# The loop order of a two-layer feed-forward stage behind attention and a Fourier mix

## The chip, the cores and the metric

One core of one Trainium2 chip. The metric is the device time in microseconds (us) of one execution. The engines are named as in the profile: PE (TensorE, with PEld for its weight loads), DVE (VectorE), ACT (ScalarE), POOL (GpSimd) and SP (SyncE, which here only issues DMAs). Each engine runs its own instructions in order and waits on semaphores for the others.

## The reference

```python
# q, k, v: (8, 12, 448, 64); w_pre, w_post: (12, 12); w_ch1: (768, 3072); w_ch2: (3072, 768)
scores = (q @ k^T) / 8                                   # per batch and head, 448 x 448
scores = einsum('bhij,hg->bgij', scores, w_pre)          # heads mixed before the softmax
attn = softmax(scores)
attn = einsum('bhij,hg->bgij', attn, w_post)             # and after it
x = (attn @ v) as (8, 448, 768)
u = x + real(fft(fft(x, axis=1), axis=2))
un = (u - mean(u)) / sqrt(var(u) + 1e-6)                 # per row
out = u + relu(un @ w_ch1) @ w_ch2
```

The two weights arrive as 64-bit floats. [...]

## The kernel before, in words

The program has two stages, one after the other.

**The mix** (`mix_phase`) makes u and writes it to DRAM (`u_scr`). Its loop runs over 192 steps, 24 for each batch, and its order on PE and DVE is written out by hand (`tc.manual_schedule`). A step has the premix matmuls (L307, PSUM tile `mx`, one buffer), the row maximum on DVE (L314), the exponential on ACT (L323), a scaling on POOL (L331, L336), the postmix matmuls (L346), a transposing copy on DVE (L357), and in some steps attention times values (L374), the transposes that turn x round (L416), a fold of two row groups on POOL (L431 to L438), and the matmuls of the Fourier transforms (L448, L462), whose results DVE adds onto `X` (L473, L475). Since `mx` has one buffer, the chain premix, maximum, exponential, next premix goes once round in each step. `convert` puts up to four DVE instructions of the weight conversion into each step: a piece is 128 x 384 weights, takes seven instructions (L512 to L523) and is stored to DRAM as `w1f` or `w2f`. There are 96 pieces. `_Evac` deals copies out of PSUM (L128 on ACT, L130 on DVE) to the engine with the smaller sum of estimated work, and each converted piece is charged to DVE there.

**The feed-forward stage** (`ffn_phase`) takes the 3584 rows in seven blocks of 512. Both products use Strassen's scheme: a product of 2 x 2 sub-blocks takes seven products of sums of sub-blocks (the list `ORDER`, with PSUM tiles `psP`, `psQ`, `psR`), so each weight also has sums of its quarters (in the first block made on DVE at L711 and L723 and stored to `w1s` and `w2s`). For each block, `first` runs through the 12 slices of a half of the hidden dimension, two at a time, and loads all of w_ch1 anew; `second` then multiplies the whole hidden activation `h` by all of w_ch2, loaded anew, and adds each finished product onto u (L838). `norm` normalises the next block's u (L746 to L753), transposes it on PE (L759), and POOL makes its sums (L766). A scheduler sets the order in this stage; before its first matmul come the load of u (L693) and `norm` of the first block.

Of the kernel before, what the change touches and what calls it, by code (L numbers as in the profile page):

```python
# [57 lines left out]

WC = 384

TB = 512
NTB = B * S // TB


def _consts():
# [23 lines left out]
    p = np.arange(GR)[:, None, None]  # L89
    at = S * np.arange(B)[:, None] + S - GR * np.arange(2) - p  # L90
    at[0, :, 0] = B * S + np.arange(B)
    return {"at": at.reshape(GR, 2 * B).astype(np.uint32), "ts": ts.astype(np.float32),
# [51 lines left out]

@with_exitstack
def mix_phase(ctx, tc, ident, q, k, v, w_pre, w_post, u_scr, weights):
# [21 lines left out]
    pcv = pool("pcv", 2)  # L168
# [36 lines left out]
    rows = cst.tile([GR, 2 * B], U32, name="rows")  # L205
# [249 lines left out]
    def emit_s2(b, pair, par):  # L455
# [10 lines left out]
        def done():  # L466
# [13 lines left out]
            for back in range(2):  # L480
                X = groups[b * NG + 2 * pair + back].pop("X")
                if back:
                    nc.gpsimd.indirect_dma_start(
                        out=u_scr[:, :],
                        out_offset=bass.IndirectOffsetOnAxis(
                            ap=rows[:GR, 2 * b + pair:2 * b + pair + 1], axis=0),
                        in_=X[:GR, :], in_offset=None)
                    continue
                u0 = b * S + i0
                nc.sync.dma_start(out=u_scr[u0:u0 + GR, :], in_=X[:GR, :])  # L490
                if n > GR:
                    nc.sync.dma_start(out=u_scr[u0 + GR:u0 + n, :], in_=X[GR:n, :])
        return [done]


    def emit_convert(src, r0, c0, dst, split):
        raw = pcv.tile([P, WC, 2], U32, name="raw64", tag="raw64")
        nc.gpsimd.dma_start(
            out=raw.rearrange("p n w -> p (n w)"),
            in_=src[r0:r0 + P, c0:c0 + WC].bitcast(U32))  # L500
        lo, hi = raw[:, :, 0], raw[:, :, 1]
        top = pcv.tile([P, WC], F32, name="top", tag="top")
        tmp = pcv.tile([P, WC], F32, name="tmp", tag="tmp")
        topb, tmpb = top[:, :].bitcast(U32), tmp[:, :].bitcast(U32)

        vec = nc.vector  # L510
        ops = [
            lambda: vec.tensor_scalar(tmpb, hi, 0x7fffffff, None, op0=ALU.bitwise_and),  # L512
            lambda: vec.tensor_scalar(tmp[:, :], tmp[:, :], _f32(0x38000000),
                                      _f32(0x47efffff), op0=ALU.max, op1=ALU.min),
            lambda: vec.tensor_scalar(topb, tmpb, 0x07ffffff, 3, op0=ALU.bitwise_and,
                                      op1=ALU.logical_shift_left),
            lambda: vec.scalar_tensor_tensor(topb, hi, 0xc0000000, topb,
                                             op0=ALU.bitwise_and, op1=ALU.bitwise_or),
            lambda: vec.tensor_scalar(tmpb, topb, 0xff800000, None,
                                      op0=ALU.bitwise_and),  # L520
            lambda: vec.scalar_tensor_tensor(tmp[:, :], lo, 2.0 ** -52, tmp[:, :],
                                             op0=ALU.mult, op1=ALU.mult),
            lambda: vec.tensor_tensor(top[:, :], top[:, :], tmp[:, :], op=ALU.add),  # L523
        ]

        def store():
            ev.d += 7 * 440.0
            nc.sync.dma_start(
                out=dst, in_=top.rearrange("p (m f) -> p m f", m=split))
        return ops, store  # L530

    cuts, conv = list(weights), []

    def convert(n):

        for _ in range(n):
            if not conv and cuts:
# [125 lines left out]
def ffn_phase(ctx, tc, ident, u_scr, w1f, w2f, w1s, w2s, out):  # L663
# [190 lines left out]
    for x in range(NT2):  # L854
        norm(0, x)
# [66 lines left out]
```

## Time and profile before

| | |
|---|---|
| median of 3 runs | 2749.06 us (2737.71 to 2753.45) |
| the profiled execution, its own time | 2746.39 us |
| its span, first to last instruction | 2744.6 us |
| mean granted TensorE clock | 0.967 |
| PE busy | 2476.4 us, 90% of the span |
| DVE busy | 1262.2 us, 46% |
| ACT busy, POOL busy | 724.0 us, 732.0 us |
| moved by DMA | 462.60 MB |

The span has a first part, the mix, in which PE and DVE are both busy over 80% of the time; a short valley between 1065 and 1158 us; and the feed-forward stage, in which PE is busy 98% of the time and DVE about a quarter. A busy share over the whole span says little: each stage has to be read by itself.

### The profile page before, as it was taken

How to read it: one execution, taken by the hardware profiler on the slowest of the kernel's cores; microseconds unless marked ns; L12 is line 12 of the kernel's file. 1: busy time of each engine (PE TensorE's matmuls, PEld its weight loads, DVE VectorE, ACT ScalarE, POOL GpSimd, SP SyncE). 2: the span in 40 equal slices, each digit the busy share in tenths (PEclk: the TensorE clock that was granted, in tenths of full speed). 3: DMA queues.
4: the chain of work that ended last, by engine and by line, in shares of the span. 5: the costliest groups of instructions: out<-in, count | busy, mean ns of one | idle time of the engine just before them, and what ended most of it. 6: DMA issues, size and time to landing. Idle time of an engine off the chain costs nothing.

```text
span 2744.6 us, 46540 instructions
## 1 busy us (share of the span) xinstructions
PE 2476.4 (90%) x18544; PEld 1587.2 (58%) x18544; DVE 1262.2 (46%) x2238; ACT 724.0 (26%) x2135; POOL 732.0 (27%) x1117
## 2 busy tenths in 40 slices
PE   4778888888888886499999999999999999999998
PEld 2334344444444443387577678668658767866865
DVE  3887888888887876543032122213203212221220
ACT  2555555555555552110011001001001100100100
POOL 5465767666665544200100010010010000001000
PEclk7999999999999998799999999999999999999999
DMA  6665657575656457744444444444445444444432
GB/s 168 181 183 173 189 168 202 164 202 164 193 175 186 152 157 252 280 161 175 141 172 165 155 155 161 161 166 161 150 155 171 157 150 167 149 163 160 144 109 107
DMA packets 184471, 462.60 MB, mean 169 GB/s; under 512 B 23111, under 2 KB 129095, under 8 KB 171712
## 3 DMA queue, kind: packets, MB, share of 16 engines
q1 hardware_dynamic: 159968, 361.30, 38.7%
q0 software_dynamic: 24288, 98.33, 13.0%
q8 instruction: 148, 2.42, 0.4%
q14 instruction: 67, 0.55, 0.1%
HBM read 317.17 MB, written 59.79 MB: 137 GB/s over the span
## 4 chain that ended last, share of the span: by engine, by line
PE 41%; issue 9%; DMA 7%; DVE 1%; POOL 0%; SPq 0%; POOLq 0%; ACT 0%
PE psP L829 12%; PE psP L789 10%; PE psR L829 7%; PE psR L789 6%; PE psQ L829 3%; DMA w1t<-w1f 3%; PE psQ L789 2%; DMA u<-u_scr 2%; DMA out_dram<-u 2%; DMA w1t<-w1s 1%; PE psQ L759 1%; DVE st L746 0%; POOL ub L766 0%; DVE u L838 0%; SPq L703 0%
## 5 line engine op out<-in xcount | busy, mean ns | idle before, releaser
L789 PE MATMUL psP<-ub,w1t 128*128 128x256 f32 x2016 | 469.3, 386 | 26.6 <-DVE mv L748 16.9
L789 PEld LDWEIGHTS psP<-ub,w1t 128*128 128x128 f32 x2016 | 385.9, 193 | 94.7 <-DMA w1t<-w1f 22.1
L829 PE MATMUL psP<-w2t,h 128*128 128x384 f32 x1344 | 436.9, 486 | 0.0
L829 PEld LDWEIGHTS psP<-w2t,h 128*128 128x128 f32 x1344 | 254.4, 190 | 173.4
L323 ACT ACTIVATE PP<-mx,nmx 128x448 f32<-128x448 f32 x384 | 239.9, 629 | 376.2 <-DVE nmx L314 372.2
L766 POOL TENSOR_TENSOR ub<-ub 128x768 f32<-128x768 f32 x28 | 50.0, 1806 | 1036.2 <-ACT ub L761 1035.6
L336 POOL TENSOR_SCALAR PP<-PP,rcp 128x448 f32<-128x448 f32 x384 | 259.6, 686 | 154.0 <-DVE rcp L333 109.4
L307 PE MATMUL mx<-Kr,kw 60*64 60x448 f32 x1536 | 204.0, 589 | 97.0 <-ACT PP L323 88.2
L357 DVE STREAM_TRANSPOSE Pv<-po 128x896 f32<-128x896 f32 x192 | 212.9, 1109 | 101.4 <-PE po L346 101.2
L789 PE MATMUL psR<-ub,w1t 128*128 128x256 f32 x1008 | 232.1, 379 | 0.5 <-DMA w1t<-w1s 0.5
L314 DVE TENSOR_REDUCE nmx<-mx 128x2 f32<-128x896 f32 x192 | 206.2, 1074 | 34.9 <-PE mx L307 23.9
L829 PE MATMUL psR<-w2t,h 128*128 128x384 f32 x672 | 220.0, 486 | 0.0
L281 PE MATMUL ms<-kT,qT 64*64 64x448 f32 (+1 forms) x1536 | 205.3, 568 | 7.0 <-DVE X L475 6.3
L374 PEld LDWEIGHTS ms<-Pv,vv 64*64 64x64 f32 x5376 | 169.4, 142 | 67.2 <-issue 38.7
L128 ACT COPY Sb<-ms 124x448 f32<-124x448 f32 x379 | 186.5, 538 | 81.1 <-PE ms L281 66.1
L789 PEld LDWEIGHTS psR<-ub,w1t 128*128 128x128 f32 x1008 | 191.2, 190 | 27.8 <-DMA w1t<-w1s 1.9
L346 PE MATMUL po<-PP,kw 60*32 60x448 f32 x3072 | 194.1, 562 | 9.1 <-DVE rcp L333 7.7
L374 PE MATMUL ms<-Pv,vv 64*64 64x120 f32 x5376 | 181.0, 278 | 16.9 <-ACT Sb L128 15.4
L838 DVE TENSOR_TENSOR u<-u,psP 128x384 f32<-128x384 f32 x56 | 31.0, 554 | 341.6 <-PE psP L829 341.6
L829 PEld LDWEIGHTS psR<-w2t,h 128*128 128x128 f32 x672 | 126.3, 190 | 84.3
L307 PEld LDWEIGHTS mx<-Kr,kw 60*64 60x64 f32 x1536 | 42.2, 135 | 207.1 <-ACT PP L323 153.9
L761 ACT COPY ub<-psQ 128x384 f32<-128x384 f32 x56 | 25.0, 481 | 508.3 <-PE psQ L759 508.3
(92 smaller groups left out, 2604.4 us busy)
## 6 DMA issues: line engine op xcount, KB each, us to landing
Kr<-Sb SPq DMA_DIRECT2D x768, 105.0 KB
w2t<-w2s SPq DMA_DIRECT2D x56, 1152.0 KB
w2t<-w2f SPq DMA_DIRECT2D x42, 1152.0 KB
w1t<-w1s SPq DMA_DIRECT2D x72, 576.0 KB
raw<-in_moe_w_ch_dram POOLq DMA_DIRECT2D x96, 384.0 KB, 4.4
w1t<-w1f SPq DMA_DIRECT2D x84, 384.0 KB
w1t<-w1f SPq DMA_DIRECT2D x96, 192.0 KB
w1t<-w1s SPq DMA_DIRECT2D x72, 192.0 KB
```

Source lines behind the costliest of these rows:

```text
L128: self.nc.scalar.copy(out=out, in_=in_)
L281: nc.tensor.matmul(pss[x][64 * y:64 * y + r0 + 64 - lo, :S], st["qT", xx][64 * x:64 * x + 64, y, lo:r0 + 64], st["kT", xx][64 * x:64 * x + ...
L307: nc.tensor.matmul(mx[64 * z:64 * z + 64, x, :S], kw1[64 * x:64 * x + KR, :], Kr[64 * x:64 * x + KR, z, :], start=True, stop=True)
L314: nc.vector.tensor_reduce(nmx[:, :], steps[T]["mx"][:, :, :S], axis=AX.X, op=ALU.max, negate=True)
L323: nc.scalar.activation(PP[:, x, :], steps[T]["mx"][:, x, :S], ACTF.Exp, bias=steps[T]["nmx"][:, x:x + 1], accum_out=den[:, x:x + 1])
L336: nc.gpsimd.tensor_scalar(PP[:, x, :], PP[:, x, :], rcp[:, x:x + 1], 1.0, op0=ALU.mult, op1=ALU.mult)
L346: nc.tensor.matmul(po[o:o + 32, z, :S], kw2[64 * z:64 * z + KR, y, :], PP[64 * z:64 * z + KR, :, c * HS:(c + 1) * HS], start=True, stop=True)
L357: nc.vector.transpose(g["Pv"][:, T % GT, :].rearrange("p (z s) -> p z s", z=2), steps[T]["po"][:, :, :S])
L374: nc.tensor.matmul(pss[y][64 * x:64 * x + 64, :nu * R], st["v"][64 * y:64 * y + 64, i, jb * D:(jb + 1) * D], _ap(Pv, 64 * y * rp + 32 * jb ...
L766: nc.gpsimd.tensor_tensor(ub[:, o], ub[:, a], ub[:, b], op=ALU.subtract)
L789: nc.tensor.matmul(p, w[m][:, i, kc, :], ub[:, i, kc, :], start=opens and kc == 0, stop=kc == NK - 1, skip_group_check=True)
L829: nc.tensor.matmul(p, lhs[i][:, half * NQ + kf, x * P:(x + 1) * P], w[:, kf, :], start=opens and half == 0 and kf == 0, stop=half == 1 and ...
```

## The change

The feed-forward loop is turned inside out. The hidden dimension is cut into six chunks; the outer loop runs over chunks, the inner one over the seven row blocks, 42 iterations in all. The seven forms of a chunk's weights (three quarters and four sums) lie in SBUF while all seven blocks pass. All of u (seven tiles) stays in SBUF, and each chunk adds its share onto it. The normalised and transposed blocks with their Strassen sums are made during chunk 0, stored to DRAM (`ub_scr`) and loaded again for every later chunk. In the last chunk each finished piece of the output is stored by itself.

The conversion moves with it. In the mix only chunk 0 is converted, at most one DVE instruction a step; the other five chunks are converted during the feed-forward stage, three DVE instructions after each product (`wts.deal(3)`). A unit is one row slice: four raw pieces of seven instructions, four sums, one store. The feed-forward order on PE and DVE is now written out by hand, u has one DRAM tensor for each batch, and its loads are issued by SP and not by POOL.

```diff
+NC = 6
+NM = DFF // 2 // P        # 12
+FM = NM // NC             # 2
+FC = FM * P               # 256
...
+class _Weights:
+    def open(self, ctx, tc):
...
+        self.praw, self.ptmp, self.pst = pool("wraw", 2), pool("wtmp", 1), pool("wst", 1)
...
+        def load(k):          # one raw piece, 256 or 384 weights wide
...
+                nc.gpsimd.dma_start(
+                    out=raws[k][:, :f, :].rearrange("p f w -> p (f w)"),
+                    in_=src.bitcast(U32))
...
+        def begin(k):
...
+            load(k + 1)
...
+        def store():
+            nc.gpsimd.dma_start(out=dst.rearrange("k p f -> p k f"),
+                                in_=box["st"][:, :, :w])
...
+    def deal(self, n):
+        while self.ops and (n > 0 or not self.ops[0][1]):
+            fn, dve = self.ops.pop(0)
+            fn()
+            n -= dve
...
 # the mix
-            ops = 0 if s < -4 else 1 if s - 1 in sums else 4
             if 0 <= s < TOT:
                 emit_postmix(s)
-                convert(min(ops, 1))
+                if s >= 4 and s % GS not in (13, 19, 0, 1):
+                    wts.deal(1)
+                    ev.d += 400.0
                 emit_turn(s)
-                ops -= 1
-            convert(ops)
...
 # the feed-forward stage
-ORDER = (0, 1, 4, 5, 2, 6, 3)
+ORDER = (0, 4, 5, 1, 6, 2, 3)
...
+    def sums(t):
+        for o, a, b in ((4, 6, 0), (5, 2, 4), (6, 2, 6), (3, 1, 5)):
+            nc.vector.tensor_tensor(ubs[t, o][:, :, :], ubs[t, a][:, :, :],
+                                    ubs[t, b][:, :, :], op=ALU.subtract)
+        for i in ORDER:
+            nc.sync.dma_start(out=ub_scr[t][i], in_=ubs[t, i][:, :, :])
...
+    def first(n):
+        c, t = divmod(n, NTB)
...
+            for m in range(FM):
+                for kc in range(NK):
+                    nc.tensor.matmul(p[:, m, :], w1[i][:, kc, m * P:(m + 1) * P],
+                                     ub[:, kc, :],
...
+            if i != 2:
+                wts.deal(3)
+            if t == NTB - 1 and c + 1 < NC:
+                load_w1(c + 1, i)
+            if NTB <= n + 1 < NC * NTB:
+                new_ub(n + 1, i)
+                nc.sync.dma_start(out=ubs[n + 1, i][:, :, :],
+                                  in_=ub_scr[(n + 1) % NTB][i])
...
+    def second(n, h):
...
+        norms = c == 0 and t + 1 < NTB
+        if norms:
+            un = norm(t + 1, 0)
...
+            if norms and k < NT2:
+                turn(t + 1, k, un)
+                if k + 1 < NT2:
+                    un = norm(t + 1, k + 1)
+                else:
+                    sums(t + 1)
+            wts.deal(3)
...
-    for t in range(NTB):
-        if t + 1 < NTB:
-            load_u(t + 1)
-        second(t, first(t))
+    with tc.manual_schedule(engines={mybir.EngineType.PE, mybir.EngineType.DVE}):
+        for n in range(NC * NTB):
+            c, t = divmod(n, NTB)
+            if c + 1 < NC and t < NK + FM:
+                wts.add(c + 1, t)
+            wts.deal(0)
+            if c == 0 and t + 2 < NTB:
+                load_u(t + 2)
+            second(n, first(n))
+            wts.deal(1000)
```

What this does to the order of instructions is seen at three places. The first is DVE in the middle of the mix. Before (L314 is the row maximum, L357 the transposing copy, L333 the softmax's reciprocal, the rest are the conversion):

```order
L333 RECIPROCAL rcp<-den 128x2
L314 TENSOR_REDUCE nmx<-mx 128x2
L523 TENSOR_TENSOR top<-top,tmp 128x384
L357 STREAM_TRANSPOSE Pv<-po 128x896
L512 TENSOR_SCALAR tmp<-raw_922 128x384
L513 TENSOR_SCALAR tmp<-tmp 128x384
L515 TENSOR_SCALAR top<-tmp 128x384
```

and after (a step like it: L441 is the maximum, L484 the transposing copy, L460 the reciprocal, L133 a copy out of PSUM, L219 and L223 the conversion):

```order
L460 RECIPROCAL rcp<-den 128x2
L441 TENSOR_REDUCE nmx<-mx 128x2
L133 COPY Sb<-ms 124x448
L219 TENSOR_SCALAR tmp<-raw_608 128x256
L484 STREAM_TRANSPOSE Pv<-po 128x896
```

Four conversion instructions between one maximum and the next have become one, narrower, and one copy out of PSUM has come over from ACT in some steps.

The second is DVE during `second`. Before, in the second block (h sums L845, additions onto u L838, the last step of `norm` L753; the statistics of `norm` stand earlier, among the instructions of `first`):

```order
L838 TENSOR_TENSOR u<-u,psQ 128x384
L845 TENSOR_TENSOR h<-h 128x1024
L753 TENSOR_SCALAR un<-u,mv,rstd 128x768
L838 TENSOR_TENSOR u<-u,psR 128x384 x2
L753 TENSOR_SCALAR un<-u,mv,rstd 128x768
L838 TENSOR_TENSOR u<-u,psP 128x384 x2
```

and after, in chunk 0 (additions onto u L873, `norm` L775 to L782, conversion L237 to L245):

```order
L873 TENSOR_TENSOR u_13365<-u_13365,psP 128x384 x2
L775 BN_STATS st<-u_13486 128x6 x2
L777 BN_AGGR mv<-st 128x2
L779 TENSOR_SCALAR rstd<-mv 128x1
L782 TENSOR_SCALAR un<-u_13486,mv,rstd 128x768
L237 TENSOR_SCALAR tmp<-wst 128x256
L241 SCALAR_TENSOR_TENSOR tmp<-raw_13784,tmp 128x256
L245 TENSOR_TENSOR wst<-wst,tmp 128x256
L873 TENSOR_TENSOR u_13365<-u_13365,psR 128x384 x2
```

A whole `norm` and three conversion instructions now stand between the additions of one product and those of the next.

The third is SP's queue between the stages. Before, POOL issued the load of u (L693), and SP held loads of w_ch2's pieces (L719, L733) and stores of its sums (L725) among the last stores of u (L490, L492):

```order
L490 DMA u_scr<-X 112x768
L492 DMA u_scr<-X 1x768
L725 DMA w2s<-w2t 128x2x384 x6
L719 DMA w2t<-w2f 128x4x384
L733 DMA w2t<-w2f 128x2304 x3
```

After, the loads of u stand on SP behind two loads of w_ch2's first chunk (`w_0_86`), whose last unit is stored by POOL when DVE has made its last sums at the very end of the mix:

```order
L616 DMA u_72<-X 112x768 x2
L618 DMA u_72<-X 1x768
L760 DMA w2t<-w_0_86 128x768 x2
L751 DMA u_13359<-u_65 128x768 x3
L751 DMA u_13359<-u_65 64x768
L751 DMA u_13359<-u_66 64x768
```

The load of u for block 0 needs only the first two batches (`u_65`, `u_66`), and stands behind a store that comes last.

More of the change, by code (lines that the diff above doesn't have):

```diff
@@ L167, in mix_phase @@
     pzz = pool("pzz")
-    pcv = pool("pcv", 2)
+    wts.open(ctx, tc)
     cst = pool("cst")
@@ L491, in done @@
                 if n > GR:
-                    nc.sync.dma_start(out=u_scr[u0 + GR:u0 + n, :], in_=X[GR:n, :])
+                    nc.sync.dma_start(out=u_scr[b][i0 + GR:i0 + n, :], in_=X[GR:n, :])
         return [done]
[L496 to L537, printed above, removed]
-                ops, store = emit_convert(*cuts.pop(0))
-                conv.extend(ops)
-                conv.append(store)
-            if conv:
-                conv.pop(0)()
-            if len(conv) == 1:
-                conv.pop(0)()
     fill = {"tile": [], "full": [], "none": []}
@@ L552, in mix_phase @@
     LG, LM = 4, 2
-    sums = set()
+    for n in range(NK + FM):
+        wts.add(0, n)
     for b in range(B):
```

360 lines of the change are left out of this document (185 added, 175 removed).

## The prediction

> **What bounds the kernel now.** I read the busy time by stage first, since the page's shares are means over stages with different limits. A row gives a stretch and its length, the busy time of PE, PEld, DVE, ACT and POOL, the granted clock, the DMA share and GB/s.
>
> ```profile
> 52.60:1064.80 1012.20, 856.96 (x12078) 415.56 (x12080) 823.58 (x1350) 556.33 (x1699) 615.97 (x985) 0.96 0.60 178
> 1064.80:1114.90 50.10, 35.58 (x330) 22.17 (x324) 32.48 (x63) 7.72 (x31) 11.25 (x13) 0.82 0.89 300
> 1114.90:1157.50 42.60, 8.64 (x37) 7.02 (x38) 18.55 (x49) 4.10 (x9) 6.50 (x8) 0.56 0.84 309
> 1157.50:2744.60 1587.10, 1551.43 (x6012) 1131.08 (x6011) 375.60 (x747) 146.80 (x383) 72.30 (x64) 0.99 0.45 154
> ```
>
> The first row runs from the first row maximum to the last, 191 step intervals, so 5.30 us a step; PE is idle for 1012.2 - 857.0 = 155.2 us of it, and DVE is busy 81%. The second is the mix's tail, the third the valley until feed-forward matmuls run steadily, the fourth the feed-forward stage, where PE is 98% busy. The change can win at most some 36 us in the fourth row, so the mix and the valley decide. What DVE does for the conversion there:
>
> ```profile
> L521 DVE SCALAR_TENSOR_TENSOR tmp<-raw,tmp 128x384 f32<-128x384 uint32 x95 | 72.2, 760 | 1.4
> L517 DVE SCALAR_TENSOR_TENSOR top<-raw,top 128x384 uint32<-128x384 uint32 x95 | 67.1, 706 | 1.4
> L523 DVE TENSOR_TENSOR top<-top,tmp 128x384 f32<-128x384 f32 x95 | 66.9, 704 | 1.2
> L513 DVE TENSOR_SCALAR tmp<-tmp 128x384 f32<-128x384 f32 x95 | 49.2, 518 | 1.9
> L519 DVE TENSOR_SCALAR tmp<-top 128x384 uint32<-128x384 uint32 x95 | 46.0, 484 | 2.1
> L515 DVE TENSOR_SCALAR top<-tmp 128x384 uint32<-128x384 uint32 x95 | 45.1, 474 | 11.5 <-DMA w1f<-top 9.6 <-DMA w2f<-top 0.9
> L512 DVE TENSOR_SCALAR tmp<-raw 128x384 uint32<-128x384 uint32 x94 | 42.2, 449 | 2.6 <-DMA raw<-in_moe_w_ch_dram 2.6
> ```
>
> Together 388.7 us in 664 instructions, 585 ns each, nearly half of DVE's 823.6. Then what PE waits for there:
>
> ```profile
> L307 PE MATMUL mx<-Kr,kw 60*64 60x448 f32 x1528 | 198.8, 587 | 88.3 <-ACT PP L323 88.2
> ...
> L258 PE MATMUL ms<-ident,rawk 128*128 128x128 f32 x147 | 24.3, 305 | 28.0 <-ACT Sb L128 25.0 <-DMA rawk<-in_k_dram 3.0
> L258 PE MATMUL ms<-ident,rawq 128*128 128x128 f32 x147 | 21.8, 281 | 8.4 <-ACT Sb L128 8.4
> ```
>
> The largest wait is the premix (L307) for the exponential, the chain that goes once round a step; the exponential in its turn waits for the maximum on DVE, which stands behind the conversion. The timeline shows it by the starts of the premix:
>
> ```profile
> 672.56 0.98 PE L307 MATMUL mx<-Kr,kw 60*64 60x448 f32 x8 [0.48 <-ACT PP L323]
> 677.85 0.98 PE L307 MATMUL mx<-Kr,kw 60*64 60x448 f32 x8 [0.58 <-ACT PP L323]
> 683.36 0.98 PE L307 MATMUL mx<-Kr,kw 60*64 60x448 f32 x8 [1.35 <-ACT PP L323]
> ...
> 1025.45 0.98 PE L307 MATMUL mx<-Kr,kw 60*64 60x448 f32 x8
> 1029.50 0.98 PE L307 MATMUL mx<-Kr,kw 60*64 60x448 f32 x8
> ```
>
> Two steps of premix, qk, attention times values and postmix took 5.29 and 5.51 us beside the conversion; one with the same PE work at the end, where the conversion is nearly over, took 4.05. But not every loss is the conversion's:
>
> ```profile
> 972.35 0.98 PE L307 MATMUL mx<-Kr,kw 60*64 60x448 f32 x8 [0.57 <-ACT PP L323]
> ...
> 976.60 0.98 PE L307 MATMUL mx<-Kr,kw 60*64 60x448 f32 x8 [1.60 <-ACT PP L323]
> ...
> 982.33 0.17 DVE L333 RECIPROCAL rcp<-den 128x2 f32<-128x2 f32 x1 [1.76 <-POOL den L331]
> ...
> 984.97 1.77 PE L307 MATMUL mx<-Kr,kw 60*64 60x448 f32 x8 [2.11 <-ACT PP L323]
> ```
>
> Here POOL works on a fold, its `den` comes late, DVE waits in order, and the step takes 8.37 us after one of 4.25.
>
> **The change, part by part.**
>
> *Conversion out of the mix.* 672 instructions become 160, at most one a step: at 585 ns about 300 us leave DVE, which then has some 2.7 us of work in a step and is no bound. What PE gets of it lies between 0 (all waits have other causes) and 155 us (all idle time). The 16 folds stay: 8.37 - 4.25 = 4.1 us each, 66 us. Of the 36.4 us at the transposes (L258), which wait for copies on ACT, I leave half, 18, since ACT gives some copies away but keeps its exponentials. So 155 - 66 - 18 = 71; I take **-70 us**, 4.9 us a step. It agrees with the pairs above: 1.2 to 1.5 us in the six or so steps of a batch that have no fold, 8 batches, about 64. The moved copies (88 of 384 `Sb` copies from ACT to DVE) cost DVE under half a microsecond a step, covered by what left it. The stores on SP and raw loads on POOL that go with the conversion wait for nothing there now, and I count nothing for them.
>
> *The tail.* The sums of w_ch2 leave it, and with them waits for their loads. One of them held DVE, and PE behind it:
>
> ```profile
> 1072.76 1.75 PE L346 MATMUL po<-PP,kw 60*32 60x448 f32 x16 [5.46 <-DVE rcp L333]
> ...
> 1114.32 0.55 DVE L475 TENSOR_TENSOR X<-X,ms 112x383 f32<-112x383 f32 x1
> ...
> 1130.65 1.61 POOL L693 DMA_DIRECT2D u<-u_scr  x2 [5.13 <-issue]
> 1145.10 1.48 DVE L746 BATCH_NORM_STATS2 st<-u 128x6 f32<-128x384 f32 x3 [9.27 <-DMA u<-u_scr]
> ```
>
> **-6 us** (0 to -12). *The valley.* From the last addition onto X (1114.32 and 0.55) to the steady feed-forward matmuls are now 42.6 us: 16 until the load of u is issued, 14 until it has landed, 12 for `norm`. After, u's load for block 0 would need none of the last batches, but on SP it stands behind two loads of w_ch2's chunk, which wait for POOL's store of the last unit, which waits for two sums on DVE after the last addition. I count 1 us for the sums, 9 for the store (1.4 MB; the 1.5 MB load of u above took 14 among others), 5 for three loads of 0.4 MB, and 11.5 for `norm`, whose sums DVE now makes: 26.5, **-16 us** (-25 if the store is quick, 0 if it takes as long as u's load and one wait more).
>
> *The feed-forward stage.* Its matmuls stay the same in number and shape:
>
> ```profile
> 1377.81 2.75 PE L789 MATMUL psP<-ub,w1t 128*128 128x256 f32 x12
> 1380.40 2.75 PE L789 MATMUL psQ<-ub,w1t 128*128 128x256 f32 x12
> ...
> 1493.70 15.64 PE L829 MATMUL psP<-w2t,h 128*128 128x384 f32 x48
> 1509.18 15.64 PE L829 MATMUL psQ<-w2t,h 128*128 128x384 f32 x48
> ...
> 1540.80 0.82 PE L759 MATMUL psQ<-ident,un 128*128 128x128 f32 x6
> 1541.45 15.65 PE L829 MATMUL psP<-w2t,h 128*128 128x384 f32 x48
> ```
>
> By the starts, 12 of `first` take 2.59 us and 48 of `second` 15.48. An iteration has 84 and 56 of them: 18.13 + 18.06 = 36.19 us, 42 times 1520, less the 2.6 done at the stage's start in my table: 1517. Transposes: 24 pairs of 0.65, 16 us. What waits come on top is DVE's part, now in strict order:
>
> ```profile
> L838 DVE TENSOR_TENSOR u<-u,psP 128x384 f32<-128x384 f32 x56 | 31.0, 554 | 341.6 <-PE psP L829 341.6
> L809 DVE TENSOR_TENSOR h<-h 128x512 f32<-128x512 f32 x42 | 29.0, 691 | 1.3
> ...
> 1147.03 0.14 DVE L750 TENSOR_SCALAR rstd<-mv 128x1 f32<-128x1 f32 x1
> ...
> 1147.25 0.58 POOL L751 TENSOR_TENSOR rstd<-rstd,mhalf 128x1 f32<-128x1 f32 x1 [14.98 <-DVE rstd L750]
> ...
> 1148.08 0.66 DVE L753 TENSOR_SCALAR un<-u,mv,rstd 128x768 f32<-128x768 f32 x1
> ```
>
> In chunks 1 to 4 `second` gives DVE 14 additions of 0.5 us (they overlap a little), one of 0.69 and 14 conversion instructions. Those are narrower and POOL is nearly idle there; I take 0.4 us: 13.3 us beside 18.06 of PE, and the last addition of each bank ends over a microsecond before PE comes back to it. I cost these iterations at nothing, and 5 us for chunk borders; the cover is gone if a conversion instruction takes over 0.7 us. In chunk 0 four `norm`s join: 1.2 for the statistics (by the row at 1145.10, three take 1.48, and one step joins them), then from 1147.03 to 1148.74 with POOL's power in the middle, so 2.9 us each, DVE standing still for POOL, 11.6; and the four block sums that were POOL's, 0.95 each by the 512-wide row, 3.8. With 1.5 us left over from `first`, DVE needs 1.5 + 11.6 + 7 + 0.7 + 3.8 + 5.6 = 30 us for a `second` in which PE needs 18.06 + 2.6 = 20.7. The transposes and the last product wait for it: 9 us in each of five iterations, 3.4 in the sixth, which converts nothing: 48 us (20 if DVE's lag is absorbed by the next `first`, 75 if `norm` takes 4). The end:
>
> ```profile
> 2736.11 0.55 DVE L838 TENSOR_TENSOR u<-u,psP 128x384 f32<-128x384 f32 x1 [3.31 <-PE psP L829]
> ```
>
> From here to the end of the span are 8.5 us, 7.9 of them the 1.5 MB store; with a store of 0.2 MB I take 4 in all (3 to 8). Sum 1517 + 16 + 5 + 48 + 4 = 1590 beside 1587: **+3 us**. What the old stage lost at block borders is given back in chunk 0.
>
> *Sum*, against the profiled execution: 2744.6 - 70 - 6 - 16 + 3 = 2655.6 of span, and 1.8 around it as now (2746.39 - 2744.6): **2657 us**. The median of the runs stands 2.7 above the profiled execution.
>
> **The rivals.** *Slower:* the raw pieces come late. A piece's seven instructions take 7/3 products of 2.59 us, 6.0 us, and its load is issued one piece ahead. If it lands later, DVE stands still in order and the additions behind it hold PE's banks.
>
> ```profile
> DMA to landing us min/median/max: 3.4/4.4/9.7
> ```
>
> These are the raw loads of before: median inside, maximum outside; DVE waited 2.6 us in all (L512 above). With 100 pieces in the feed-forward stage it decides from 0.9 us of lateness a piece, if all of it reaches PE: a landing of 6.9 us. At 7.2 us the time is 2777. Against it: the stage moves 154 GB/s now and needs less later. The Trainium skill, page SBUF — State Buffer, section SBUF: two separate sides, speaks for it: a DMA issued by POOL gets its descriptors from POOL, which DVE's two-port instructions lock out, and 0.62 us became 3.1. By that figure the median would be an estimated 6.9 us, and the time an estimated 2747. No run here shows the delay alone, and the row of 2.6 us was taken with DVE 81% busy.
>
> *Faster:* POOL's folds shorten too, since DVE no longer holds it up, and chunk 0's lag is partly absorbed: 110 in the mix and 30 in the stage instead of 48 give 2599. For it speaks that the fold's neighbours were converter instructions; against it that the step of 8.37 us shows POOL alone on the way.
>
> *Less:* the waits in the mix stay, because copies on ACT and additions onto X set them and not the conversion: -20 instead of -70, 2707. For it: the 36 us of L258 and only a few steps like the pair compared.
>
> **How the numbers follow.** Forecast (2625 to 2690) 0.52; faster rival 0.18; less 0.18; slower 0.07; the rest 0.05. The range 2600 to 2710 cuts off the slower rival and half of the faster. A measurement of this kernel tells about 0.5%, 14 us. Below 2735: 0.91; within: 0.04; above: 0.05.
>
> **What the new profile would show.** Premix starts 4.9 us apart in the mean and 4.0 to 4.2 in steps without fold, with folds still near 8; the valley under 30 us with `w2t` ahead of u; iterations of 36.2 us in chunks 1 to 5 and 46 in chunk 0, PE's waits there naming `un` and the last additions. I am wrong if iterations of later chunks exceed 37 us, if DVE's wait for `raw` comes to more than 20 us, or if the premix stays over 5.2 us apart.

## The result, and the profile after

The changed kernel takes 2653.28 us, the median of 4 runs (2651.71 to 2660.46), against 2750.45 us for the kernel before on the same chip: a ratio of 0.966, with a 95% interval of 0.9625 to 0.9696. The prediction was 2657. The profiled execution took 2654.14 us with a span of 2652.4, so the span lost 92.2 us.

The same four stages as in the table of before (length; busy time of PE, PEld, DVE, ACT, POOL; granted clock; DMA share; GB/s):

```profile
49.60:999.80 950.20, 850.26 (x12116) 408.20 (x12117) 605.85 (x934) 503.63 (x1595) 526.69 (x914) 0.97 0.46 141
999.80:1043.40 43.60, 31.67 (x298) 20.23 (x282) 22.45 (x43) 7.61 (x31) 12.54 (x17) 0.88 0.17 51
1043.40:1070.20 26.80, 8.12 (x37) 6.78 (x38) 9.73 (x24) 3.73 (x8) 4.18 (x6) 0.55 0.78 260
1070.20:2652.40 1582.20, 1544.64 (x6013) 1128.87 (x6011) 867.16 (x1820) 199.50 (x342) 92.02 (x146) 1.00 0.44 141
```

| stage | before | after | difference | predicted |
|---|---|---|---|---|
| up to the first row maximum | 52.6 | 49.6 | -3.0 | not counted |
| mix, 191 steps | 1012.2 | 950.2 | -62.0 | -70 |
| tail | 50.1 | 43.6 | -6.5 | -6 |
| valley | 42.6 | 26.8 | -15.8 | -16 |
| feed-forward | 1587.1 | 1582.2 | -4.9 | +3 |
| span | 2744.6 | 2652.4 | -92.2 | -89 |

In the mix a step takes 4.97 us instead of 5.30. PE is idle for 99.9 us of it (950.2 - 850.3) instead of 155.2, and DVE is busy 64%. PE's two waits on which the prediction rested, in groups of that stretch:

```profile
L434 PE MATMUL mx<-Kr,kw 60*64 60x448 f32 x1529 | 196.1, 573 | 38.6 <-ACT PP L450 34.2 <-DMA Kr<-Sb 4.0
...
L385 PE MATMUL ms<-ident,rawk 128*128 128x128 f32 x147 | 23.9, 302 | 27.1 <-ACT Sb L131 10.5 <-DVE Sb L133 6.2 <-DVE qT L133 4.5
```

The premix (now L434) waits 38.6 us instead of 88.3; the transposes of k (L385) wait 27.1 instead of 28.0, so these hardly moved. Single steps, by the starts of the premix:

```profile
661.96 0.98 PE L434 MATMUL mx<-Kr,kw 60*64 60x448 f32 x8
666.06 0.98 PE L434 MATMUL mx<-Kr,kw 60*64 60x448 f32 x8
669.88 0.98 PE L434 MATMUL mx<-Kr,kw 60*64 60x448 f32 x8 [0.33 <-ACT PP L450]
...
675.00 0.97 ACT L131 COPY Sb<-ms 124x448 f32<-124x448 f32 x2 [1.47 <-DMA Kr<-Sb]
675.59 0.99 PE L385 MATMUL ms<-ident,rawk 128*128 128x128 f32 x7 [2.06 <-ACT Sb L131]
...
676.51 0.98 PE L434 MATMUL mx<-Kr,kw 60*64 60x448 f32 x8
```

Steps of 4.10 and 3.82 us stand beside one of 6.63. In it POOL begins a fold, and PE waits 2.06 us for ACT's copy of scores (`Sb`), which itself waits 1.47 us for its buffer, until SP's gather of earlier scores (`Kr<-Sb`) has read it.

The valley, in the order of time. The w2t loads are issued on SP only when the last unit's store has landed, and u's nine pieces come behind them:

```profile
1042.81 0.55 DVE L602 TENSOR_TENSOR X<-X,ms 112x383 f32<-112x383 f32 x1
1043.27 1.02 DVE L249 TENSOR_TENSOR wst<-wst 128x384 f32<-128x384 f32 x2
1044.59 0.98 POOL L252 DMA_DIRECT2D w<-wst  x1 [2.25 <-DVE wst L249]
...
1051.43 0.82 SPq L760 DMA_DIRECT2D w2t<-w  x2
1052.30 6.42 SPq L751 DMA_DIRECT2D u<-u  x9
1058.41 1.02 DVE L775 BATCH_NORM_STATS2 st<-u 128x6 f32<-128x384 f32 x2 [14.12 <-DMA u<-u]
...
1070.17 2.75 PE L818 MATMUL psR<-ub,w1t 128*128 128x256 f32 x12
```

An iteration of chunk 0, from one first `first` matmul (1161.83) to the next (1207.99), and two iteration starts of chunk 1:

```profile
1161.83 2.75 PE L818 MATMUL psP<-ub,w1t 128*128 128x256 f32 x12
...
1184.11 0.85 PE L791 MATMUL psQ<-ident,un 128*128 128x128 f32 x6 [1.41 <-DVE un L782]
...
1192.65 0.84 PE L791 MATMUL psQ<-ident,un 128*128 128x128 f32 x6 [1.42 <-DVE un L782]
...
1198.70 1.01 PE L791 MATMUL psQ<-ident,un 128*128 128x128 f32 x6 [2.11 <-DVE u L873]
...
1207.99 2.32 PE L818 MATMUL psP<-ub,w1t 128*128 128x256 f32 x10
...
1490.12 2.75 PE L818 MATMUL psP<-ub,w1t 128*128 128x256 f32 x12
...
1526.31 2.75 PE L818 MATMUL psP<-ub,w1t 128*128 128x256 f32 x12
```

In chunk 0 an iteration takes 46.16 us here (47.16, 46.17, 47.59 and 47.59 from the second to the fifth); the transposes, which wait for `un` and for DVE's additions onto u, are nearly all that is added. In its `second`, from 1179.96, DVE is busy 24.15 of 28.03 us (the third figure behind the length; PE and PEld come first) and stands 3.0 more for POOL's power:

```profile
1179.96:1207.99 28.03, 22.14 (x81) 12.68 (x80) 24.15 (x54) 4.12 (x9) 4.34 (x7) 1.00 0.35 127
```

In chunk 1 an iteration takes 36.19 us, and so do all those from the last one of chunk 0 on, by their starts, across the chunk borders too. At the end of the span the last product starts at 2645.62; with its 2.74 us it leaves 4.0 to the end.

### The profile page after: what moved, and what is told of

Read it like the earlier page. It is cut to its first block, busy times and chain, and to the rows that moved or that the text cites. A ratio compares the mean times of both kernels' runs of the same rounds, so it can differ in the third digit from the quotient of the medians.

```text
span 2652.4 us, 47290 instructions
## 1 busy us (share of the span) xinstructions
PE 2454.0 (93%) x18544; PEld 1575.4 (59%) x18544; DVE 1514.2 (57%) x2842; ACT 723.5 (27%) x1989; POOL 660.0 (25%) x1129
## 4 chain that ended last, share of the span: by engine, by line
PE 74%; DVE 9%; POOL 5%; DMA 4%; ACT 3%; issue 2%; SPq 1%; POOLq 0%; ACTq 0%; DVEq 0%
PE psP L818 16%; PE psP L867 15%; PE psR L818 8%; PE psR L867 7%; PE mx L434 4%; PE psQ L818 4%; PE ms L501 4%; PE po L473 4%; PE psQ L867 4%; PE ms L408 3%; DMA Kr<-Sb 2%; PE ms L589 2%; ACT PP L450 2%; DVE nmx L441 2%; PE ms L575 2%
## 5 line engine op out<-in xcount | busy, mean ns | idle before, releaser
L867 PE MATMUL psP<-w2t,h 128*128 128x384 f32 x1344 | 464.2, 489 | 1.9 <-DVE u L873 1.9
L202 POOL DMA_DIRECT2D raw<-in_moe_w_ch_dram x120 | 69.3, 577 | 923.6 <-DVE tmp L241 904.7
L484 DVE STREAM_TRANSPOSE Pv<-po 128x896 f32<-128x896 f32 x192 | 213.6, 1112 | 131.7 <-PE po L473 131.2
L463 POOL TENSOR_SCALAR PP<-PP,rcp 128x448 f32<-128x448 f32 x384 | 246.4, 652 | 132.3 <-DVE rcp L460 124.7
L441 DVE TENSOR_REDUCE nmx<-mx 128x2 f32<-128x896 f32 x192 | 207.5, 1081 | 119.4 <-PE mx L434 118.1
L873 DVE TENSOR_TENSOR u<-u,psP 128x384 f32<-128x384 f32 x336 | 182.5, 553 | 144.5 <-PE psP L867 141.9
L434 PE MATMUL mx<-Kr,kw 60*64 60x448 f32 x1536 | 198.0, 574 | 49.0 <-ACT PP L450 34.2
L823 ACT COPY h<-psP 128x512 f32<-128x512 f32 x42 | 24.6, 585 | 767.9 <-PE psP L818 767.9
L867 PE MATMUL psR<-w2t,h 128*128 128x384 f32 x672 | 230.5, 486 | 0.0
L829 DVE TENSOR_TENSOR h<-h,psQ 128x512 f32<-128x512 f32 x42 | 28.9, 688 | 299.5 <-PE psQ L818 293.8
L501 PEld LDWEIGHTS ms<-Pv,vv 64*64 64x64 f32 x5376 | 161.0, 136 | 62.3 <-issue 37.1
L501 PE MATMUL ms<-Pv,vv 64*64 64x120 f32 x5376 | 172.5, 271 | 15.8 <-ACT Sb L131 15.4
L131 ACT COPY Sb<-ms 124x448 f32<-124x448 f32 x296 | 146.9, 537 | 32.9 <-DMA Kr<-Sb 12.6
```

The source lines that it names most:

```text
L131: self.nc.scalar.copy(out=out, in_=in_)
L434: nc.tensor.matmul(mx[64 * z:64 * z + 64, x, :S], kw1[64 * x:64 * x + KR, :], Kr[64 * x:64 * x + KR, z, :], start=True, stop=True)
L441: nc.vector.tensor_reduce(nmx[:, :], steps[T]["mx"][:, :, :S], axis=AX.X, op=ALU.max, negate=True)
L463: nc.gpsimd.tensor_scalar(PP[:, x, :], PP[:, x, :], rcp[:, x:x + 1], 1.0, op0=ALU.mult, op1=ALU.mult)
L484: nc.vector.transpose(g["Pv"][:, T % GT, :].rearrange("p (z s) -> p z s", z=2), steps[T]["po"][:, :, :S])
L501: nc.tensor.matmul(pss[y][64 * x:64 * x + 64, :nu * R], st["v"][64 * y:64 * y + 64, i, jb * D:(jb + 1) * D], _ap(Pv, 64 * y * rp + 32 * jb ...
```

## The experiments

Each was timed beside the kernel before on the same chip, but not all on one chip: before had medians of 2746.4 to 2754.4 us, so rows are best compared by the ratio. The table gives the median, the ratio to before, and from each profiled execution four lengths in us: a mix step (from the first row maximum to the last, by 191), the tail (from the last row maximum to the end of the last addition onto X), the valley's first part (from there to the first `first` matmul), and the second to fifth iterations of chunk 0. An iteration without any wait is 36.19 + 2.6 for its transposes = 38.8 us.

| kernel | median us | ratio, 95% interval | step | tail | to first product | chunk 0 |
|---|---|---|---|---|---|---|
| before | 2750 | 1 | 5.300 | 50.0 | 37.7 | |
| after | 2653.3 | 0.966, 0.9625 to 0.9696 | 4.975 | 43.6 | 21.7 | 46.2 to 47.6 |
| before_one_a_step | 2709.2 | 0.9868, 0.984 to 0.9896 | 5.113 | 54.3 | 37.2 | |
| conv_in_mix | 2890.0 | 1.0511, 1.0476 to 1.0547 | 6.325 | 50.5 | 13.1 | 42.2 |
| conv_early | 2659.5 | 0.9668, 0.9637 to 0.9699 | 5.037 | 43.1 | 13.9 | 46.2 to 48.0 |
| fold_on_dve | 2642.4 | 0.9593, 0.9559 to 0.9626 | 4.947 | 43.5 | 21.8 | 46.2 to 47.6 |
| no_conv_ffn | 2636.7 | 0.9585, 0.9553 to 0.9617 | 5.003 | 42.6 | 21.5 | 42.2 to 42.4 |
| wst_two | 2655.1 | 0.9651, 0.9625 to 0.9676 | 4.953 | 45.5 | 21.2 | 46.2 to 47.6 |
| stats_early | 2636.1 | 0.9582, 0.9555 to 0.9609 | 4.962 | 46.2 | 21.4 | 42.5 to 44.2 |
| stats_balanced | 2653.7 | 0.9655, 0.9623 to 0.9688 | 5.015 | 46.4 | 21.2 | 45.8 to 49.7 |
| stats_spread | 2621.5 | 0.9511, 0.9491 to 0.953 | 4.992 | 44.9 | 22.0 | 40.5 to 40.9 |
| u_first | 2652.1 | 0.9628, 0.9602 to 0.9654 | 4.981 | 45.9 | 16.6 | 46.2 to 48.1 |
| best | 2641.3 | 0.9628, 0.9595 to 0.9661 | 4.948 | 41.3 | 17.6 | 45.8 to 49.1 |
| best_spread | 2606.1 | 0.9456, 0.9436 to 0.9477 | 4.951 | 43.4 | 17.2 | 40.5 to 40.9 |

Seven of these kernels (after, no_conv_ffn, wst_two, stats_early, stats_balanced, stats_spread, u_first) have the same mix. Their steps range from 4.953 to 5.015 with a mean of 4.983, 12 us from end to end over 191 steps, and their tails from 42.6 to 46.4: a difference smaller than that is not read off one profile.

### Is the mix's gain the conversion?

**before_one_a_step**: the loops of before, and a sixth of its conversion (the DVE instructions that make 32-bit floats of the weights' 64-bit ones).

```diff
-    cuts, conv = list(weights), []
+    every, cuts, conv = list(weights), [], []
+    for sp in sorted({e[4] for e in every}):
+        same = [e for e in every if e[4] == sp]
+        for n in range(0, len(same), 6):
+            src, r0, c0, _, _ = same[n]
+            cuts.append((src, r0, c0, [e[3] for e in same[n:n + 6]], sp))
...
-            ops = 0 if s < -4 else 1 if s - 1 in sums else 4
+            ops = 1 if s >= 4 and s % GS not in (13, 19, 0, 1) else 0
```

> The kernel before, its loops as they were, with 16 of the 96 pieces converted, one DVE instruction a step; each converted piece is stored to six places, so that the stores stay 96 and five sixths of the weights are left out. Theory (the 62 us of the attention stage come from the conversion that is no longer there): a step goes from 5.30 to 4.95 to 5.03 us, the stage loses 52 to 67 us, the tail 0 to 7, the feed-forward stage keeps its length: 2752 - 64 = 2688 us, 2675 to 2700. Rival (they come from the other queues, buffers and order of the new attention stage; six instructions a step cost conv_in_mix most of its time at one buffer, not on DVE): a step stays above 5.2 us, time above 2735.

A step takes 5.113 us, 35.6 us less over the mix, between the theory and its rival. What PE waits for in that mix:

```profile
L307 PE MATMUL mx<-Kr,kw 60*64 60x448 f32 x1528 | 203.7, 582 | 38.4 <-ACT PP L323 33.3 <-DMA Kr<-Sb 4.5
...
L258 PE MATMUL ms<-ident,rawk 128*128 128x128 f32 x147 | 25.4, 317 | 41.0 <-DVE Sb L130 17.3 <-ACT Sb L128 14.5 <-DVE qT L130 5.0
```

The premix's wait falls from 88.3 to 38.4 us, as far as in the changed kernel (38.6). So the chain that the prediction named is shown: with the loops of before, taking conversion out is enough for all that the premix gained. The transposes went the other way: k's wait 41.0 us here, 28.0 in before, 27.1 in the changed kernel. They wait for copies of `Sb`, and these for their buffers. Such waits of before, in its mix (total us, times, longest):

```profile
ACT Sb L128 <- DMA Kr<-Sb: 11.6, 4, 5.6
```

And of before_one_a_step:

```profile
DVE Sb L130 <- DMA Kr<-Sb: 25.7, 6, 8.5
...
ACT Sb L128 <- DMA Kr<-Sb: 23.6, 6, 7.1
```

They grew from 11.6 to 49.3 us. In the changed kernel they are in between:

```profile
ACT Sb L131 <- DMA Kr<-Sb: 12.6, 4, 5.5
DVE Sb L133 <- DMA Kr<-Sb: 9.3, 3, 6.9
```

The experiment may have a part in this itself: it puts six stores at a time on SP, the gathers' queue, where the changed kernel has none. It shows 36 of the 62 us as the conversion's. Of the remaining 26 PE idles 20 (120.1 us in this mix, 99.9 in the changed kernel), nearly all of it at the transposes and at attention times values, and is busy 6 longer. It stands 27 us above the changed kernel in gather waits (49.3 - 21.9), which fits in size, but such waits don't set a step's length by themselves: in the seven kernels with the same mix they range from 21.9 to 36.3 us, and wst_two, with 31.6, has the shortest step. What the 26 us are stays open.

**conv_in_mix**: the opposite way, all conversion back into the changed kernel's mix.

```diff
-    for n in range(NK + FM):
-        wts.add(0, n)
+    for c in range(NC):
+        for n in range(NK + FM):
+            wts.add(c, n)
...
-                    wts.deal(1)
+                    wts.deal(6)
```

> The changed kernel with all 30 conversion units put back into the attention stage, six DVE instructions a step instead of one, and none in the feed-forward stage; the new loops stay. Theory (conversion in the attention stage is what held its steps at 5.3 us, and conversion in chunk 0 is most of chunk 0's lag): a step goes from 4.97 back to about 5.3 us, +62 us; the tail gets back some 7 us; chunk 0 loses 13 us of DVE work an iteration and its lag falls from 44 us to about 10, -34. Sum 2653 + 62 + 7 - 34 = 2688 us, 2670 to 2705. Rival (the steps got shorter through the new placing of tiles and transfers, not through the missing conversion): steps stay under 5.1 us and the time falls to about 2620.

It came out 202 us above the theory, and the edit made a wait that I had overlooked. A unit is now 32 instructions, dealt in 5 steps, and there is one `wst`:

```profile
PE po L473 <- DVE rcp L460: 188.4, 67, 10.1
...
DVE wst L227 <- DMA w<-wst: 151.1, 28, 9.1
```

DVE stands 151 us in the mix at the first write of a unit until the last one's store has landed, in front of the reciprocal that PE's postmix waits for. Of the mix's 258 us (1208.2 - 950.2) 107 are left for 800 more instructions, 0.13 us each; the change's 512 fewer (672 to 160) for 62 us are 0.12 each. In before_one_a_step 560 fewer (672 to 112) gave 36 us, 0.06 each. So the direction is the theory's, but with a subtraction of that size no price of one instruction follows. In the same run chunk 0's iterations without conversion are 42.2 us.

**conv_early**: chunk 0's conversion two instructions a step, so that it ends half-way.

```diff
-                    wts.deal(1)
-                    ev.d += 400.0
+                    if wts.ops:
+                        wts.deal(2)
+                        ev.d += 800.0
```

> The changed kernel with chunk 0's conversion dealt two instructions a step from the same first step, so that it ends near the middle of the attention stage and the second half has none. Theory: the cost in the attention stage is about 0.08 us of a step for each instruction a step (0.33 us for some four), so the first half's steps grow by 0.08 us, the second half's shrink by as much, no net change there; the last store is long done when the last fold comes, so the w2t loads leave SP early and u's loads stand behind nothing: the valley falls from 27 to 16 to 18 us, the tail by 0 to 3; time about 2642 us. Rival (u's loads wait for the last scatter of X and not for the queue): valley within 2 us of 27, time 2651 to 2655.

The valley did what the theory says (13.9 instead of 21.7 us), the mix didn't: 12 us longer. The last four batches, which have no conversion but for the first six steps, took 5.22, 5.20, 5.11 and 4.97 us a step, against 4.97, 5.10, 5.01 and 5.13 with one instruction. So no gain shows where the last instruction of a step went. But the gather waits are high again:

```profile
ACT Sb L131 <- DMA Kr<-Sb: 33.2, 9, 8.4
DVE Sb L133 <- DMA Kr<-Sb: 21.5, 6, 7.0
```

Of these 54.7 us, 43.0 lie in the last four batches, where the changed kernel has under 4. They can hide what the missing instruction gave, so its price can't be read off. What makes the gathers later in one kernel than in another stays open.

**fold_on_dve**: the fold's five instructions with `nc.vector` in place of `nc.gpsimd` (L558 to L565).

> The changed kernel with the fold's five instructions moved from POOL to DVE. Theory (what is left of the PE waits in the attention stage is mostly the fold that holds POOL's scalings back, two steps near 6.8 us for each of 16 folds instead of 4.1): on DVE five passes of 0.5 to 0.9 us, 3 us a fold; the two steps together shrink by 2 to 4.5 us, 16 times, 30 to 70 us; time about 2605, 2580 to 2625. Rival (DVE takes its instructions in order, so a fold there waits for the X copies and holds the maxima behind it): the step with the fold stays above 6.3 us, time within 15 us of 2653 or above it.

The rival held. On DVE an addition of the fold takes 965 ns where POOL took 1820, and the three kernels with it have steps of 4.947, 4.948 and 4.951, all below the seven with the fold on POOL: 0.034 us a step under their mean, 6.5 us in all. DVE's waits for POOL's `den` fell from 90.9 to 19.1 us in the mix, yet the premix's wait for the exponential only from 34.2 to 25.6. The long steps change place: by batch position (mean over the middle six batches) three steps of 4.80, 7.42 and 6.84 us became 7.18, 4.45 and 6.23. Most of their length is PE's own work. The three together in one batch, of the changed kernel and of this one (length, PE busy first):

```profile
487.03:506.43 19.40, 16.59 (x194) 8.06 (x186) 12.54 (x23) 9.74 (x24) 16.37 (x25) 1.00 0.37 110
481.57:500.15 18.58, 15.85 (x152) 7.23 (x148) 15.40 (x28) 9.94 (x24) 12.95 (x23) 0.91 0.45 127
```

PE is idle for 2.8 us in the first and 2.7 in the second. So moving the fold gains little. It doesn't show what a mix without any fold would take, since on DVE the fold stands in the same chain.

### What makes chunk 0 late?

**no_conv_ffn**: `wts.add(c + 1, t)` taken out, all chunks load chunk 0's weights.

> The changed kernel without any conversion in the feed-forward stage; chunks 1 to 5 read the converted weights of chunk 0, so those weights are left out of the result. Theory (conversion beside the normalisation makes DVE late in chunk 0): iterations of chunk 0 go from 46 to 38 us, its lag from 44 to about 10 us, later iterations stay at 36.19 us; time about 2619 us. Rival A (normalisation and transposes alone pace chunk 0): iterations stay above 44 us, time above 2643. Rival B (conversion also costs time in chunks 1 to 5): iterations there fall under 36.0 us.

Neither number: 42.2 us. Conversion is 4 to 5.4 us of an iteration's excess over 38.8, `norm` the other 3.4, which is what the sixth iteration, without conversion, takes in the changed kernel as well (42.19). Later iterations stayed at 36.19 us, so the conversion costs nothing there.

**wst_two**: `pool("wst", 2)` in the feed-forward stage.

> The changed kernel with two buffers for the converted unit (wst) in the feed-forward stage instead of one. Theory (in chunk 0 DVE, late already, stands 6.6 us an iteration at the first write of the next unit, until the store of the last one has landed): the iterations of 46 to 47.6 us fall to 43 to 44, time 15 to 25 us down, 2633. Rival (the DVE work itself, 36 us an iteration, sets the pace): they stay above 46 us, time above 2648.

The wait went and nothing was gained: 46.2 to 47.6 us, as in the changed kernel. In the iteration from 1114.67 the changed kernel's DVE stood 6.6 us for `wst`; in the same iteration here it stands as long for PE:

```profile
DVE h L829 <- PE psQ L818: 6.7, 1, 6.7
DVE un L782 <- POOL rstd L780: 3.0, 4, 0.8
```

The wait lay at the iteration's start, beside `first`, where DVE is early.

**stats_early**: the statistics and powers of the next block during `first`, only the scaling (L782) between the products of `second`.

```diff
             if i != 2:
                 wts.deal(3)
+            if c == 0 and t + 1 < NTB and i in (5, 1, 6, 2):
+                x = (5, 1, 6, 2).index(i)
+                stats[t + 1, x] = stat(t + 1, x)
```

> The changed kernel with the four blocks' statistics and powers (L775 to L780) of the next row block done during the first product of chunk 0; only the scaling L782 stays between the products of the second. Theory (2.9 us for each norm in the second product, with POOL's power in its chain, hold the transposes back): 2.2 us of each norm leave the second product, 6 to 8 us an iteration; chunk 0's iterations fall from 47 to 40 or 41 us, its lag from 44 to 10 to 15 us, time about 2620. Rival (DVE's work over the whole iteration and the wait for wst set it, wherever the statistics stand): under 2 us an iteration, time above 2643.

Half of it: 42.5 to 44.2 us, 17 us in the median. What is left is mostly one wait, that of the first transposes:

```profile
1220.17 0.84 PE L798 MATMUL psQ<-ident,un 128*128 128x128 f32 x6 [2.41 <-DVE un L789]
1223.43 0.82 PE L798 MATMUL psQ<-ident,un 128*128 128x128 f32 x6
```

The first row waits 2.41 us for its `un`, the next for nothing. That gave two opposite ideas of where the conversion belongs.

**stats_balanced**: more of it in `first`.

```diff
-                wts.deal(3)
+                wts.deal(4 if c == 0 else 3)
...
-            wts.deal(3)
+            wts.deal(3 if c or k >= NT2 else 0)
```

> stats_early, and in chunk 0 four conversion instructions after each of six products of the first kind, none after the first four products of the second kind, three after the rest. Theory (what is left of the lag is the conversion between the second kind's products that have a norm beside them: wst_two took its wait away and gained nothing, because that wait lies beside first products where DVE has slack): chunk 0's iterations fall from 43.3 to 39.5 to 41 us, time 2636 - 15 = 2621 us, 2612 to 2628. Rival (DVE's total of 36 us with little slack left, now late in the first products): above 43 us, time 2634 or above.

Wrong, and 17.6 us slower than stats_early. DVE falls behind in `first`; its last product and then the first transposes wait for the backlog:

```profile
1235.14 2.86 PE L825 MATMUL psP<-ub,w1t 128*128 128x256 f32 x12 [2.01 <-DVE h L839]
1244.59 1.34 PE L798 MATMUL psQ<-ident,un 128*128 128x128 f32 x6 [4.02 <-DVE un L789]
```

Two things lie in that backlog: the six more instructions, and the wait for the single `wst`, on which DVE stands 9.7, 4.6, 4.5 and 5.5 us in the second to fifth iterations, against 7.5, 2.2, 2.1 and 4.8 in stats_early. That wait was free in the changed kernel, where `first` had slack; here it needn't be. The runs don't separate the two.

**stats_spread**: less of it in `first`, over six iterations, all five units of chunk 1 added at once, and two `wst` buffers (`wts.open(ctx, tc, 2)`).

```diff
-                wts.deal(3)
+                wts.deal(3 if c else 2)
...
-            wts.deal(3)
+            wts.deal(3 if c else (3, 3, 3, 2, 1, 1, 2)[k])
...
+            for m in range(NK + FM):
+                if c + 1 < NC and t == (m if c else 0):
+                    wts.add(c + 1, m)
```

> stats_early with chunk 1's 160 conversion instructions spread over six iterations of chunk 0 instead of five, 12 in the first products and 15 in the second (27 an iteration, was 32 with 18 first), and two buffers for wst, since the unit's end now falls anywhere. Theory (in stats_early PE loses 2.4 us where the first transposes wait for DVE to end the backlog of the first products, and stats_balanced put 6 instructions more there and lost 4 to 5 us more; what counts is the number of DVE instructions before the first scaling): chunk 0's iterations fall from 43.3 to 39 to 41 us, time 2636 - 16 = 2620 us, 2612 to 2628. Rival (the conversion between the second products holds the transposes wherever it is dealt): above 42.5 us, time above 2631.

The forecast held: 40.5 to 40.9 us, and the first transposes wait 0.4 us:

```profile
1173.96 0.84 PE L798 MATMUL psQ<-ident,un 128*128 128x128 f32 x6 [0.40 <-DVE un L789]
```

Three things changed at once: 6 fewer instructions in `first` (with 1 more in `second`), 27 instead of 32 in the iteration, and no wait for `wst` any more. Which of them gave how much wasn't tested.

### The valley, and a faster kernel

**u_first**: SP's order at the start of the stage set by hand.

```diff
+    with tc.manual_schedule(engines={mybir.EngineType.SP}):
+        for t in range(2):
+            load_u(t)
+        for i in ORDER:
+            load_w2(0, i)
```

> The changed kernel with SP's order set by hand at the feed-forward stage's start: the loads of u's first two row blocks, then all seven w2t loads (before: two w2t loads, which wait for the last converted unit's store, then u). Theory (SP takes its DMAs in order, so u's loads stood behind that store although their rows were written long ago): from the end of the last X addition to the first w1t product 14 us instead of 21.7, time 2653 - 8 = 2645 us. Rival (the loads wait for the rows themselves or for DMA bandwidth): 20 us or more, time 2651 or above.

The place is right, the size is not: 16.6 us to the first product, 5 less, and another 1 us given back in the first iteration. u's loads now leave 2.4 us after the last addition (1049.43 against 1047.08), where it was 8.9, and take 7.6 us instead of 6.1 to land:

```profile
1049.43 8.58 SPq L751 DMA_DIRECT2D u<-u  x9
...
1056.99 1.02 DVE L775 BATCH_NORM_STATS2 st<-u 128x6 f32<-128x384 f32 x2 [8.98 <-DMA u<-u]
```

In the median no difference can be told from the changed kernel.

**best** joins stats_balanced, u_first and fold_on_dve, **best_spread** the same with stats_spread.

> stats_balanced with u_first's order on SP and the fold on DVE. Theory (the three act at different places and add up): 2621 - 6 - 6 = 2609 us, 2598 to 2620. Rival (the valley's gain is lost again in chunk 0's first iteration, as 1 of 5 us was in u_first, and the attention stage varies by 4 us between runs anyway): no more than 5 us under stats_balanced.

> stats_spread with u_first's order on SP and the fold on DVE. Theory (best stood 12 us under stats_balanced, 17.9 of them before the first product and some from the attention stage's own variation): 10 us under stats_spread, 2610 us, 2600 to 2620. Rival (those 12 us were mostly variation): within 5 us of stats_spread.

The 17.9 us named there are the two profiles' difference at the end of the last addition onto X (1053.3 and 1035.3 us). best stood 12 us under stats_balanced but, with stats_balanced in it, 32 above its forecast. best_spread takes 2606.08 us (2600.75 to 2610.49), 15.4 under stats_spread and 47 under the changed kernel (by the ratios, 2.0% of before); of the 15.4, 4.8 are the way to the first product, and the profiles show 7.8 in the mix, about as much as the fold gave in the mean. Its valley and its feed-forward stage:

```profile
1037.70:1058.50 20.80, 6.60 (x25) 5.34 (x26) 9.41 (x27) 2.87 (x6) 4.62 (x7) 0.59 0.92 322
1058.50:2608.70 1550.20, 1539.91 (x6025) 1130.37 (x6023) 864.44 (x1820) 200.40 (x344) 91.51 (x146) 1.00 0.45 144
```

PE is idle for 10.3 us of that stage, where it was 37.6 in the changed kernel.

## Why the prediction was right

*The mix, -70, measured -62.* The mechanism is the one described: steps without a fold come down to 4 us, the premix's wait fell by 50 of 88 us, and taking conversion out of before lowered that wait as far and gave 36 us by itself. But the size came out near partly by luck, since the working had its parts wrong and they cancelled. The 66 us left to the folds are 16 times a difference between two steps' lengths, taken out of PE's idle time. In that pair PE's busy time (the figure behind the length) differs too:

```profile
972.35:976.60 4.25, 2.65 (x33) 0.69 (x33) 4.18 (x8) 2.52 (x8) 3.26 (x3) 1.00 1.03 270
976.60:984.97 8.37, 4.66 (x40) 1.84 (x40) 5.69 (x8) 2.72 (x8) 6.87 (x10) 0.96 0.77 224
```

PE is idle for 1.60 us in the first step and 3.71 in the second: 2.1 us a fold, 34 in all. With 34 the same sum gives 155 - 34 - 18 = 103 us. Of the 18 us that I took from the transposes' wait 5.5 came (36.4 to 30.9 us, 27.1 of them for k), and a wait grew that I hadn't looked at: copies of `Sb` that wait for a gather, 11.6 to 21.9 us. PE idles 99.9 us, where I had left 85. Of the 62 us, 55.3 are idle time, the premix's 50 and the transposes' 5.5, and 6.7 are busy time (857.0 to 850.3), a term that the sum didn't have.

*The tail, -6, measured -6.5*: no run tests its cause, seven equal tails range over 3.8 us, and before_one_a_step's, with less conversion, is longer than before's (54.3). *The valley, -16, measured -15.8*, term by term: sums and issue 1.2 us (predicted 1), the store 6.8 to the w2t issue (9), from u's issue to its landing 6.1 (5), from there to steady matmuls 11.8 (11.5). u_first shows that the queue order and no missing row held u's loads.

*The feed-forward stage, +3, measured -4.9.* The 1520 us of the matmuls and 16 of the transposes are there to a tenth of a microsecond an iteration. Chunk 0's lag over 38.8 us is 8.3 in the first iteration (`second` of it took 28.96 us where I had 30), then 8.4, 7.4, 8.8, 8.8 and 3.4: 45 against 48. The chunk borders cost nothing instead of 5, and the end 4.0. That DVE's work in `second` sets it in the changed kernel is shown from both sides: less of it there is faster (no_conv_ffn, stats_early), and its wait elsewhere is free (wst_two). What I didn't see is that `first` becomes narrow in its turn: with the statistics and six more instructions there, and the wait for `wst`, stats_balanced is 3.4 to 5.4 us an iteration slower than stats_early.

*The slower rival* needed raw pieces that land 6.9 us after their issue:

```profile
DMA to landing us min/median/max: 2.9/3.5/6.0
```

DVE waited for them once, 9.0 us in the tail. These loads are of 256 and 384 KB; those of 384, the size of before, have a median of 3.9 us. By the page SBUF — State Buffer of the Trainium skill, section SBUF: two separate sides, the median would have been an estimated 6.9 us. The trace doesn't agree: 3.5. *The faster rival* had 110 us from the mix, where 62 came, and chunk 0's lag partly absorbed; it isn't, since DVE is early again at the start of each iteration and stands there (6.6 us in the one from 1114.67). *That the mix keeps its waits* holds for the transposes, not for the premix.

## What to carry to other kernels

When work leaves an in-order engine, count the time that its successors wait for it now, and then look for the next releaser in the same place: here the waits for gathers grew as DVE's work left. Take what remains out of idle time as idle time: a step that is 4.1 us longer can be idle for only 2.1 of them. Whether a wait matters depends on the half of the loop in which it stands: 6.6 us beside idle time cost nothing, while work put ahead of the one row that PE needs made iterations 3.4 to 5.4 us longer. Put side work where the engine has slack until its next deadline, by a count of instructions up to that deadline and not over the whole iteration.

## What the hardware showed besides

The same instruction takes longer in the stage in which POOL works. A conversion instruction of 256 elements in the changed kernel's mix:

```profile
L241 DVE SCALAR_TENSOR_TENSOR tmp<-raw,tmp 128x256 f32<-128x256 uint32 x12 | 7.6, 633 | 0.0
...
L223 DVE TENSOR_SCALAR tmp<-tmp 128x256 f32<-128x256 f32 x12 | 5.4, 452 | 0.0
```

and from 1120 to 2600 us, where POOL does next to nothing:

```profile
L241 DVE SCALAR_TENSOR_TENSOR tmp<-raw,tmp 128x256 f32<-128x256 uint32 x56 | 23.7, 424 | 1.4
...
L223 DVE TENSOR_SCALAR tmp<-tmp 128x256 f32<-128x256 f32 x55 | 16.1, 292 | 1.4
```

That is 1.5 times as long in both, so moving the conversion made it cheaper as well as hiding it. The Trainium skill, page SBUF — State Buffer, section SBUF: two separate sides, speaks of a port pair that DVE and POOL lock against each other. The trace agrees in direction; no run here takes POOL's work away alone. With the fold moved from POOL to DVE the first of the two took 597 ns in the mix.

The granted clock was 0.55 in the valley of the changed kernel and 0.59 in that of best_spread, as it was 0.56 before. The first matmuls behind the stretch in which PE has nothing to do are slower with it: in the changed kernel six transposes took 1.54 us from 1061.59, at a granted clock of 0.50 (1060 to 1065 us), and 0.85 us from 1184.11, at 1.00.
